# Converting the second layer's two weight matrices in turn, spread over the tiles on both sides of the layers' border

## The chip, the cores and the metric

The kernel runs on one core of one Trainium2 chip. The metric is the device time of one execution in microseconds (us). Before the change the median of three timed runs is 1086.88 us (1084.77 to 1090.79). Besides the timed runs there is one profiled execution, from which every row below is taken.

## The reference, cut to what matters

A delta-rule attention is followed by two feed-forward layers on its output. Each layer multiplies 3072 tokens of 384 features with a 384x2048 matrix, applies a function, and multiplies with a 2048x384 matrix:

```python
x = attention(q, k, v, beta)                 # 3072 tokens x 384
h = x @ moe_w_in                             # layer 1
x = (h * (1.0 / (1.0 + np.exp(-1.702 * h)))) @ moe_w_out
h = np.maximum(x @ moe2_w_in, 0.0)           # layer 2
out = (h * h) @ moe2_w_out
```

The kernel receives the four weight matrices in 64-bit form, so each must be brought to 32 bits on the chip before TensorE can use it, and each is split into a high and a low part.

## The kernel before, in words

**Tiles and steps.** The tokens are worked in six tiles of 512 per layer. A tile is 16 steps, one for each block `f` of 128 of the 2048 inner features. A step (`step`, which calls `layer2` for the step before it) gives TensorE 9 matmuls into a buffer `h` (3 blocks of features, each as high x high, low x high, high x low) and 9 matmuls into the three accumulators `z`, for the step before. Between the two lies a chain: ScalarE makes `g` from `h`, VectorE multiplies it up (`g<-g,h`), ScalarE rounds it to `ghi`, VectorE subtracts to get `glo`. There are two buffers of `h`, `g`, `ghi` and `glo`; the names in the rows carry no buffer number or, in the lists of the order, one such as `g_82` and `g_83`. TensorE's order within a step of the stretch below is three matmuls of the step's own `h`, three of the next step's `h`, three more of its own, then nine of `z`; the matmuls of the next step's `h` need a buffer that `g<-g,h` of the step before has read.

**Conversion of weights.** A matrix is converted in 16 parts of 128x384 (`split_w`). SyncE loads a part's 64-bit form into one of three buffers `raw` (`load_w`). Then ScalarE makes `c0` from it (`c<-raw` on ACT), VectorE makes two halves of `c1` (two `TENSOR_SCALAR` `c<-raw`), VectorE joins them (`c<-c,c`), ScalarE writes the high part (`vi_hi` of the first matrix of layer 2, `wo_hi` of the second), and GpSimd or VectorE, whichever the planner finds free, subtracts to get the low part (`vi_lo`, `wo_lo`). The second matrix of layer 2 takes the place of that of layer 1 in `wo_hi` and `wo_lo`, part by part, so part `f` can be written only when layer 1's last tile has used its old content. The first has storage of its own. The input of layer 2's first tile is split into `x_hi` and a low part that lies in `wi_lo`, since layer 1's first matrix is no longer needed there after four steps of the last tile.

**What sets the order.** The program does not fix the order on each engine by hand. `Program.add` collects operations with their dependencies and assumed costs; `Program.flush` then runs a plan in assumed time and issues, on each engine, the operation that is ready and was added first. An engine executes in exactly this order, and waits where a real dependency is not met. Before the change the 16 parts of the first matrix are added one behind each step of layer 1's last tile, those of the second one behind each step of layer 2's first tile. As nothing but loads, buffers and the storage holds a part back, the planner moves every part to the front as far as the three `raw` buffers allow.

Of the kernel before, what the change touches and what calls it, by code (L numbers as in the profile page):

```python
# [23 lines left out]
NF = DFF // 128  # L24
# [5 lines left out]
TUNE = dict(  # L30
    fused=4,
    warm=(10, 6),
    burst=(6, 4, 220),
    blocks=(0, 1, 2, 3),
    ja=4,
    depth=2,
    half=8,
    slack=0.0,
# [12 lines left out]
class Program:  # L51
# [8 lines left out]
    def __init__(self, queues):  # L60
        self.queues = queues
        self.ops = []
        self.writer, self.readers = {}, {}
        self.free = {q: 0.0 for q in queues}
        self.dma_free = 0.0
        self.urgent = False
        self.columns = {}
        self.run = self.run_end = self.burst_end = 0.0

    def add(self, queue, cost, fn, reads=(), writes=(), early=0, nbytes=0, after=(), cold=None):  # L70
        n = len(self.ops)
        deps = set(after)
        for k in reads:
            if k in self.writer:
                deps.add(self.writer[k])
        for k in writes:
            if k in self.writer:
                deps.add(self.writer[k])
            deps.update(self.readers.get(k, ()))
        for k in reads:  # L80
            self.readers.setdefault(k, []).append(n)
        for k in writes:
            self.writer[k], self.readers[k] = n, []
        queue = (queue,) if isinstance(queue, str) else queue
        cost = cost if isinstance(cost, tuple) else (cost,)
        self.ops.append([queue, cost, fn, deps, n - early, nbytes, None, self.urgent, cold])
# [102 lines left out]
def kernel(  # L189
# [14 lines left out]
    w1_in, w1_out, w2_in, w2_out = (w.bitcast(I32) for w in (w1_in, w1_out, w2_in, w2_out))  # L204
    pg = Program({"pe": nc.tensor, "act": nc.scalar, "dve": nc.vector, "pool": nc.gpsimd, "sp": nc.sync})
# [17 lines left out]
    wo_hi = main.tile([128, NF, DM], F32R, name="wo_hi")  # L223
    wo_lo = main.tile([128, NF, DM], F32R, name="wo_lo")
# [7 lines left out]
    NR = 3  # L232
# [73 lines left out]
    def load_w(src, f):  # L306
        s = n_conv[0] % NR
        n_conv[0] += 1
        dma(raw_sb[s], src[:, f].rearrange("p (n two) -> p n two", two=2), [], [("raw", s)], 128 * DM * 8)

    def split_w(key, f, hi, lo):
        s, t = n_conv[1] % NR, n_conv[1] % 2
        n_conv[1] += 1
        raw, c0, c1 = raw_sb[s], c0_sb[0], c1_sb[t]
        r16 = raw.rearrange("p n two -> p (n two)").bitcast(U16).rearrange("p (n q) -> p n q", q=4)
        c16 = c1.bitcast(U16).rearrange("p (n q) -> p n q", q=2)
        act(DM, [("raw", s)], ["c0"], out=c0, in_=raw[:, :, 1].bitcast(F32), scale=2.0**-112)
        ts(DM, [("raw", s)], [("c1", t, 0)], out=c16[:, :, 0], in0=r16[:, :, 1], scalar1=13, op0=ALU.logical_shift_right)
        ts(DM, [("raw", s)], [("c1", t, 1)], out=c16[:, :, 1], in0=r16[:, :, 3], scalar1=2**15, op0=ALU.bitwise_and)
        both = [("c1", t, 0), ("c1", t, 1)]  # L320
        stt(DM, ["c0"] + both, both, out=c1.bitcast(I32), in0=c0.bitcast(I32), scalar=3, in1=c1.bitcast(I32),
            op0=ALU.logical_shift_left, op1=ALU.bitwise_or)
        act(DM, both, [(key, f, 0)], out=hi[:, f, :], in_=c1)
        tt(DM, both + [(key, f, 0)], [(key, f, 1)], lo[:, f, :], c1, hi[:, f, :], ALU.subtract,
           ("pool", "dve") if n_conv[1] <= TUNE["lo_both"] else "pool")
# [363 lines left out]
    def split_x(b, c0, n):  # L689
        for c in range(KX):  # L690
            src, hi, lo = xf_sb[:, c, c0:c0 + n], x_hi[b][:, c, c0:c0 + n], x_lo[b][:, c, c0:c0 + n]
            keys = xf_keys(c, c0, n)
            K = [[("x", b, c, half, i) for half in halves_of(c0, n)] for i in range(2)]
            act(n, keys, K[0], out=hi, in_=src)
            tt(n, keys + K[0], K[1], lo, src, hi, ALU.subtract)
# [22 lines left out]
    def step(ph, j, f, c0=0, n=TT, b=0, mid=()):  # L718
        p = ns[0] % 2
        ns[0] += 1  # L720
        parts = range(2)
        if n == TT:
            ns[2] += ns[2] % 2
            s, o = ns[2] // 2 % NG, 0
            ns[2] += 2
        else:
            s, o = ns[2] // 2 % NG, CT * (ns[2] % 2)
            parts = [ns[2] % 2]
            ns[2] += 1
        W, halves = ("wi", "vi")[ph - 1], halves_of(c0, n)  # L730
        ps = h_ps[p][:, :n]
        for c in range(KX):
            wh = w_in_of[ph][0][:, f, 128 * c:128 * c + 128]
            wl = w_in_of[ph][1][:, f, 128 * c:128 * c + 128]
            hi, lo = x_hi[b][:, c, c0:c0 + n], x_lo[b][:, c, c0:c0 + n]
            mms(3 * 0.000423 * n, [(ps, wh, hi, c == 0, False), (ps, wh, lo, False, False), (ps, wl, hi, False, c == KX - 1)],
                [(W, f, 0), (W, f, 1)] + [("x", b, c, half, i) for half in halves for i in range(2)], [("h", p)])
        for todo in mid:
            todo()
        g, hi, lo = (x[s][:, o:o + n] for x in (g_sb, ghi_sb, glo_sb))  # L740
        kg, khi, klo = ([(x, s, i) for i in parts] for x in ("g", "ghi", "glo"))
        if ph == 1:
            act(n, [("h", p)], kg, out=g, in_=ps, func=AF.Tanh, scale=GATE / 2)
            stt(n, [("h", p)] + kg, kg, out=g, in0=g, scalar=1.0, in1=ps, op0=ALU.add, op1=ALU.mult)
        else:
            act(n, [("h", p)], kg, out=g, in_=ps, func=AF.Relu)
            tt(n, [("h", p)] + kg, kg, g, g, ps, ALU.mult)
        act(n, kg, khi, out=hi, in_=g)
        tt(n, kg + khi, klo, lo, g, hi, ALU.subtract)
        prev.append((ph, j, f, c0, n, hi, lo, khi + klo))  # L750
        while len(prev) > (1 if n == TT else TUNE["depth"]):
            layer2(*prev.pop(0))
# [5 lines left out]
    def convert(todo, load, n, key=None):  # L758
        for _ in range(n):
            if todo:  # L760
                _, key, f, hi, lo = todo.pop(0)
                split_w(key, f, hi, lo)
            if load:
                load_w(*(load[0][0], load.pop(0)[2]))

    with tc.manual_schedule():
# [111 lines left out]
        vi_hi = p2.tile([128, NF, DM], F32R, name="vi_hi")  # L878
        vi_lo = p2.tile([128, NF, DM], F32R, name="vi_lo")
# [6 lines left out]
        def load_z(j):  # L886
            for c in range(KX):
                dma(xf_sb[:, c], zd[128 * c:128 * c + 128, TT * j:TT * j + TT], [("zd", j, c)], xf_keys(c, 0, TT), 128 * TT * 4)

        w2i = [(w2_in, "vi", f, vi_hi, vi_lo) for f in range(NF)]  # L890
        w2o = [(w2_out, "wo", f, wo_hi, wo_lo) for f in range(NF)]
        ni, no = list(w2i), list(w2o)
        convert([], ni, NR)
        for f in range(NF):
            if f == 2:
                load_z(0)
            step(1, 5, f)
            convert(w2i, ni, 1)
        for key in [("x", 1, c, half, 1) for c in range(KX) for half in range(2)]:
            pg.readers[key] = [r for k in x_lo_keys for r in pg.readers.get(k, [])]  # L900
        split_x(1, 0, TT)
        while w2i:
            convert(w2i, ni, 1)
        for j in range(6):
            for f in range(NF):
                step(2, j, f, b=(j + 1) % 2)
                if j == 0:
                    if f == 0:
                        convert([], no, NR)
                    convert(w2o, no, 1)  # L910
                if f == 1 and j < 5:
                    load_z(j + 1)
                if f == 12 and j < 5:
                    split_x(j % 2, 0, TT)
# [69 lines left out]
```

## Time and profile before

| | |
|---|---|
| median of the runs, range | 1086.88 us, 1084.77 to 1090.79 |
| profiled execution, its own time | 1084.37 us |
| its span, first to last instruction | 1082.7 us |
| TensorE busy | 1024.4 us, 95% |
| VectorE busy | 589.6 us, 54% |
| ScalarE busy | 528.5 us, 49% |
| GpSimd busy | 332.9 us, 31% |

The time of the profiled execution is 1.67 us longer than its span. A share of busy time is a mean over stages; the share of an engine within a stage can be quite another.

### The profile page before, as it was taken

What the parts mean: (1) busy time and instruction counts of PE and PEld (TensorE: products, weight loads), DVE (VectorE), ACT (ScalarE), POOL (GpSimd) and SP (SyncE); (2) the same over time, 40 slices, a digit from 0 to 9 for tenths busy, and PEclk for the clock granted to TensorE, in tenths of its full rate; (3) what the DMA queues carried; (4) which work ended last, traced back from release to release, by engine and by line L of the source; (5) the groups of instructions that cost most, each with busy time, mean ns of one, the idle gap of its engine ahead of it and who ended that gap; (6) DMA issues with size and microseconds to landing.
All of it is one profiled execution on the core that took longest, in us unless ns stands there. A gap on an engine that the chain in (4) does not pass through costs nothing.

```text
span 1082.7 us, 23994 instructions
## 1 busy us (share of the span) xinstructions
PE 1024.4 (95%) x9900; PEld 832.9 (77%) x9900; DVE 589.6 (54%) x1122; ACT 528.5 (49%) x1088; POOL 332.9 (31%) x673
## 2 busy tenths in 40 slices
PE   4789899999999999999999989999999999999998
PEld 3778777867778787878788867788888888888886
DVE  6787886574655546453744799634333343433332
ACT  4586675636464546455544656534233242332323
POOL 1254251786647382847280144100000000000000
PEclk7798999999999999999999999999999999999999
DMA  8364462313223122212110566201001010000000
GB/s 225 98 170 133 139 174 61 113 31 93 57 60 101 60 56 88 64 51 73 50 34 5 172 179 169 94 0 59 1 7 53 1 59 1 1 30 1 30 1 29
DMA packets 43981, 76.32 MB, mean 70 GB/s; under 512 B 6624, under 2 KB 19552, under 8 KB 43872
## 3 DMA queue, kind: packets, MB, share of 16 engines
q1 hardware_dynamic: 43776, 74.75, 23.6%
q8 instruction: 77, 1.26, 0.5%
q14 instruction: 32, 0.26, 0.1%
q10 hardware_dynamic: 96, 0.05, 0.0%
HBM read 64.16 MB, written 9.44 MB: 68 GB/s over the span
## 4 chain that ended last, share of the span: by engine, by line
PE 66%; DVE 16%; ACT 8%; issue 4%; POOL 3%; DMA 2%; SPq 1%; DVEq 0%; ACTq 0%; POOLq 0%
PE h L300 28%; PE z L300 28%; PE a L300 9%; DVE c L287 3%; ACT G L273 3%; DVE kT_sb L293 2%; DVE glo L283 2%; DVE c L290 2%; DVE gu L293 1%; DVE g L290 1%; POOL tmpp L544 1%; DVE v_sb L283 1%; POOL U L547 1%; ACT gu L268 1%; DVE x_lo L283 1%
## 5 line engine op out<-in xcount | busy, mean ns | idle before, releaser
L268 ACT ACTIVATE g<-h 128x512 f32<-128x512 f32 (+1 forms) x200 | 115.5, 579 | 266.0 <-PE h L300 264.7
L300 PE MATMUL z<-glo,wo_hi 128*128 128x512 f32 (+1 forms) x600 | 231.8, 386 | 5.6 <-DVE glo L283 5.6
L300 PE MATMUL z<-ghi,wo_hi 128*128 128x512 f32 (+1 forms) x600 | 232.0, 387 | 0.1
L300 PE MATMUL z<-ghi,wo_lo 128*128 128x512 f32 (+1 forms) x600 | 229.7, 383 | 0.0
L283 DVE TENSOR_TENSOR glo<-g,ghi 128x512 fp32r<-128x512 f32 (+1 forms) x200 | 137.7, 689 | 98.6 <-ACT ghi L268 98.0
L268 ACT ACTIVATE ghi<-g 128x512 fp32r<-128x512 f32 (+1 forms) x200 | 122.6, 614 | 134.4 <-DVE g L290 68.5
L283 DVE TENSOR_TENSOR g<-g,h 128x512 f32<-128x512 f32 x96 | 66.1, 688 | 172.4 <-ACT g L268 172.4
L300 PE MATMUL h<-x_hi,wi_hi 128*128 128x512 f32 (+1 forms) x312 | 129.9, 416 | 18.3 <-DVE g L290 15.1
L544 POOL TENSOR_TENSOR tmpp<-U,gu 128x126 f32<-128x126 f32 (+22 forms) x248 | 113.2, 457 | 95.8 <-DVE U L287 77.0
L300 PEld LDWEIGHTS z<-glo,wo_hi 128*128 128x128 f32 x600 | 113.7, 189 | 33.2 <-DVE glo L283 11.8
L300 PEld LDWEIGHTS z<-ghi,wo_hi 128*128 128x128 f32 x600 | 113.6, 189 | 24.0 <-ACT ghi L268 0.9
L300 PEld LDWEIGHTS z<-ghi,wo_lo 128*128 128x128 f32 x600 | 113.7, 190 | 21.5
L290 DVE SCALAR_TENSOR_TENSOR g<-g,h 128x512 f32<-128x512 f32 (+1 forms) x104 | 66.5, 640 | 105.1 <-ACT g L268 104.9
L300 PE MATMUL h<-x_lo,wi_hi 128*128 128x512 f32 (+1 forms) x312 | 118.8, 381 | 3.2 <-DVE x_lo L283 3.2
L300 PE MATMUL h<-x_hi,wi_lo 128*128 128x512 f32 (+1 forms) x312 | 118.7, 380 | 0.4 <-DVE wi_lo L283 0.4
L300 PE MATMUL h<-x_hi,vi_hi 128*128 128x512 f32 x288 | 112.4, 390 | 0.8 <-PE h L300 0.8
L300 PE MATMUL h<-x_hi,vi_lo 128*128 128x512 f32 x288 | 112.2, 390 | 0.0
L547 POOL TENSOR_TENSOR U<-U,tmpp 128x126 f32<-128x126 f32 (+22 forms) x248 | 102.8, 415 | 20.4 <-DVE U L287 1.3
L300 PEld LDWEIGHTS h<-x_hi,wi_hi 128*128 128x128 f32 x312 | 59.7, 191 | 42.3 <-DVE g L290 24.7
L300 PEld LDWEIGHTS h<-x_hi,wi_lo 128*128 128x128 f32 x312 | 60.0, 192 | 11.6 <-DVE wi_lo L283 0.6
L300 PEld LDWEIGHTS h<-x_lo,wi_hi 128*128 128x128 f32 x312 | 60.1, 192 | 11.2 <-DVE x_lo L283 4.4
L273 ACT ACTIVATE ws<-a 32x384 f32<-32x384 f32 x92 | 44.3, 482 | 49.6 <-PE a L300 45.2
(117 smaller groups left out, 1451.4 us busy)
## 6 DMA issues: line engine op xcount, KB each, us to landing
raw<-in_w_in SPq DMA_DIRECT2D x32, 384.0 KB, 3.5
raw<-in_w_out SPq DMA_DIRECT2D x32, 384.0 KB, 3.4
kq<-in_kq SPq DMA_DIRECT2D x44, 256.0 KB, 3.0
kT_sb<-in_kq SPq DMA_DIRECT2D x11, 512.0 KB, 3.7
k_sb<-in_kt SPq DMA_DIRECT2D x12, 384.0 KB, 4.5
v_sb<-in_vt SPq DMA_DIRECT2D x12, 384.0 KB, 3.2
xf_sb<-zd SPq DMA_DIRECT2D x18, 256.0 KB, 2.7
out<-zs SPq DMA_DIRECT2D x18, 256.0 KB, 2.0
```

Of the source, the lines that this page charges most:

```text
L268: pg.add("act", c_act(n), lambda e: e.activation(**kw), reads, writes, early)
L273: e.activation(out=out, in_=in_, func=AF.Copy)
L283: pg.add(queue, cost, lambda e: e.tensor_tensor(out=out, in0=in0, in1=in1, op=op), reads, writes, early)
L287: pg.add("dve", c_dve(n, True), lambda e: e.tensor_scalar(**kw), reads, writes, early)
L290: pg.add("dve", c_dve(n), lambda e: e.scalar_tensor_tensor(**kw), reads, writes, early)
L293: pg.add("dve", c_dve(n), lambda e: e.transpose(out=out, in_=in_), reads, writes)
L300: e.matmul(out=out, lhsT=lhsT, rhs=rhs, start=start, stop=stop)
L544: e.tensor_tensor(out=t, in0=U[:, lo:hi, j:j + 1].to_broadcast(shape), in1=gu[:, j + 1:, j:j + 1].rearrange("p i o -> p o i").to_broadcast ...
L547: e.tensor_tensor(out=U[:, lo:hi, j + 1:], in0=U[:, lo:hi, j + 1:], in1=t, op=ALU.add)
```

## The change

The parts of the two matrices are put into one list in turn (first matrix part 0, second matrix part 0, first matrix part 1, ...), loaded and converted in that order. A function `spread`, called behind each step of layer 1's last tile and of layer 2's first tile (32 steps, numbered 0 to 31 here), adds the conversions that are due: part `f` of the first matrix behind step `int(1.8 f)`, part `f` of the second two steps later. That is two parts behind each of the steps 3, 5, 7, 9, 12, 14, 16, 18, 21, 23, 25 and 27, and one behind each of 0, 1, 2, 10, 11, 19, 20 and 29. While such a part is added, `gate` makes its operations depend, in the plan, on the last operation of that step. This dependency enters the plan's times alone; the conversion's instructions get no wait on a matmul from it.

```diff
+    spread=1.8,
...
+        self.gate = ()
...
-        deps = set(after)
+        deps = set(after) | set(self.gate)
...
-        w2i = [(w2_in, "vi", f, vi_hi, vi_lo) for f in range(NF)]
-        w2o = [(w2_out, "wo", f, wo_hi, wo_lo) for f in range(NF)]
-        ni, no = list(w2i), list(w2o)
-        convert([], ni, NR)
+        w2 = [x for f in range(NF) for x in ((w2_in, "vi", f, vi_hi, vi_lo), (w2_out, "wo", f, wo_hi, wo_lo))]
+        w2_load = list(w2)
+        starts = []
+
+        def spread():
+
+            starts.append(len(pg.ops) - 1)
+            while w2:
+                at = int(TUNE["spread"] * w2[0][2]) + 2 * (w2[0][1] == "wo")
+                if at >= len(starts):
+                    break
+                pg.gate = starts[at:at + 1]
+                convert(w2, (), 1)
+                pg.gate = ()
+                convert((), w2_load, 1)
+
+        convert([], w2_load, NR)
         for f in range(NF):
             if f == 2:
                 load_z(0)
             step(1, 5, f)
-            convert(w2i, ni, 1)
+            spread()
...
         split_x(1, 0, TT)
-        while w2i:
-            convert(w2i, ni, 1)
         for j in range(6):
             for f in range(NF):
                 step(2, j, f, b=(j + 1) % 2)
                 if j == 0:
-                    if f == 0:
-                        convert([], no, NR)
-                    convert(w2o, no, 1)
+                    spread()
```

The change moves rows on all engines from layer 1's last tile on. Three places on VectorE show how; names are as explained above, and `x2` stands for two instructions alike.

VectorE in steps 8 and 9 of layer 1's last tile, before the change:

```order
L290 SCALAR_TENSOR_TENSOR g_82<-g_82,h_67 128x512
L290 SCALAR_TENSOR_TENSOR c_92<-c_91,c_92 128x384
L283 TENSOR_TENSOR glo_86<-g_82,ghi_84 128x512
L287 TENSOR_SCALAR c_93<-raw_89 128x384 x2
L290 SCALAR_TENSOR_TENSOR c_93<-c_91,c_93 128x384
L287 TENSOR_SCALAR c_92<-raw_90 128x384 x2
L290 SCALAR_TENSOR_TENSOR g_83<-g_83,h_68 128x512
L290 SCALAR_TENSOR_TENSOR c_92<-c_91,c_92 128x384
L283 TENSOR_TENSOR glo_87<-g_83,ghi_85 128x512
```

The same two steps after the change:

```order
L292 SCALAR_TENSOR_TENSOR g_82<-g_82,h_67 128x512
L292 SCALAR_TENSOR_TENSOR c_92<-c_91,c_92 128x384
L285 TENSOR_TENSOR glo_86<-g_82,ghi_84 128x512
L292 SCALAR_TENSOR_TENSOR g_83<-g_83,h_68 128x512
L289 TENSOR_SCALAR c_93<-raw_88 128x384
L285 TENSOR_TENSOR glo_87<-g_83,ghi_85 128x512
L289 TENSOR_SCALAR c_93<-raw_88 128x384
L289 TENSOR_SCALAR c_92<-raw_89 128x384
L292 SCALAR_TENSOR_TENSOR c_93<-c_91,c_93 128x384
L289 TENSOR_SCALAR c_92<-raw_89 128x384
```

Before, two parts stand in every step; now two parts stand in two steps, and between `glo` of step 8 and `g` of step 9 there is nothing.

VectorE at the start of the stretch, steps 2 and 3, where the low part of layer 2's first input (`wi_lo<-xf_sb,x_hi`, three pieces) is made too, before the change:

```order
L290 SCALAR_TENSOR_TENSOR g_82<-g_82,h_67 128x512
L287 TENSOR_SCALAR c_92<-raw_88 128x384 x2
L290 SCALAR_TENSOR_TENSOR c_92<-c_91,c_92 128x384
L283 TENSOR_TENSOR glo_86<-g_82,ghi_84 128x512
L287 TENSOR_SCALAR c_93<-raw_89 128x384 x2
L290 SCALAR_TENSOR_TENSOR c_93<-c_91,c_93 128x384
L287 TENSOR_SCALAR c_92<-raw_90 128x384 x2
L283 TENSOR_TENSOR wi_lo<-xf_sb,x_hi_7279 128x512
L290 SCALAR_TENSOR_TENSOR g_83<-g_83,h_68 128x512
```

The same place after the change, from the same `g` on:

```order
L292 SCALAR_TENSOR_TENSOR g_82<-g_82,h_67 128x512
L285 TENSOR_TENSOR vi_lo<-c_92,vi_hi 128x384
L289 TENSOR_SCALAR c_92<-raw_89 128x384
L285 TENSOR_TENSOR glo_86<-g_82,ghi_84 128x512
L289 TENSOR_SCALAR c_93<-raw_88 128x384 x2
L289 TENSOR_SCALAR c_92<-raw_89 128x384
L292 SCALAR_TENSOR_TENSOR c_93<-c_91,c_93 128x384
L285 TENSOR_TENSOR wi_lo<-xf_sb,x_hi_7279 128x512 x2
L292 SCALAR_TENSOR_TENSOR c_92<-c_91,c_92 128x384
L292 SCALAR_TENSOR_TENSOR g_83<-g_83,h_68 128x512
L289 TENSOR_SCALAR c_93<-raw_90 128x384 x2
L285 TENSOR_TENSOR wi_lo<-xf_sb,x_hi_7279 128x512
```

Here the rows have not thinned out: two parts and two pieces of the input's low part now stand between one `glo` and the next `g`.

VectorE in step 23, in layer 2's first tile, where nothing but the steps' own rows stands before:

```order
L283 TENSOR_TENSOR g_83<-g_83,h_68 128x512
L283 TENSOR_TENSOR glo_87<-g_83,ghi_85 128x512
L283 TENSOR_TENSOR g_82<-g_82,h_67 128x512
L283 TENSOR_TENSOR glo_86<-g_82,ghi_84 128x512
```

The same place after the change:

```order
L285 TENSOR_TENSOR g_83<-g_83,h_68 128x512
L285 TENSOR_TENSOR glo_87<-g_83,ghi_85 128x512
L289 TENSOR_SCALAR c_93<-raw_88 128x384 x2
L289 TENSOR_SCALAR c_92<-raw_89 128x384
L292 SCALAR_TENSOR_TENSOR c_93<-c_91,c_93 128x384
L289 TENSOR_SCALAR c_92<-raw_89 128x384
L285 TENSOR_TENSOR wo_lo<-c_93,wo_hi 128x384
L292 SCALAR_TENSOR_TENSOR c_92<-c_91,c_92 128x384
L285 TENSOR_TENSOR g_82<-g_82,h_67 128x512
L285 TENSOR_TENSOR vi_lo<-c_92,vi_hi 128x384
L285 TENSOR_TENSOR glo_86<-g_82,ghi_84 128x512
```

Two parts have come in, and both of their low parts stand on VectorE; over the whole stretch VectorE has 9 of the 32 low parts now, where it had 3, and GpSimd has 23 where it had 29.

## Rows read from the trace of the kernel before

**Rows 1.** The page's 40 slices of 27 us, busy tenths.

```profile
PE   4789899999999999999999989999999999999998
DVE  6787886574655546453744799634333343433332
```

**Rows 2.** Stretch; busy us (instructions) of PE, PEld, DVE, ACT, POOL; clock; DMA share; GB/s.

```profile
613.00:688.00 75.00, 68.71 (x279) 50.62 (x278) 73.01 (x125) 47.08 (x95) 31.17 (x28) 1.00 0.62 173
688.00:763.00 75.00, 75.00 (x332) 62.10 (x331) 28.92 (x43) 28.83 (x50) 1.01 (x1) 1.00 0.09 32
```

**Rows 3.** The chain that ended last, by line, between 617 and 687 us.

```profile
by line: DVE c L287 42.3%; issue 22.7%; DVE c L290 12.2%; DVE glo L283 12.0%; DVE g L290 5.7%; DVE x_lo L283 1.9%; ACT c L268 1.6%; DVE wi_lo L283 0.9%; PE z L300 0.7%; DVEq L290 0.5%; DVEq L287 0.2%; DVEq L283 0.2%; ACT wo_hi L268 0.1%
```

**Rows 4.** VectorE's timeline through one step: start us, us, instruction.

```profile
651.73 0.68 DVE L283 TENSOR_TENSOR glo<-g,ghi 128x512 fp32r<-128x512 f32 x1
652.33 1.47 DVE L287 TENSOR_SCALAR c<-raw 128x384 uint16<-128x384 uint16 x2
653.90 0.56 DVE L290 SCALAR_TENSOR_TENSOR c<-c,c 128x384 int32<-128x384 int32 x1
654.38 0.65 DVE L287 TENSOR_SCALAR c<-raw 128x384 uint16<-128x384 uint16 x2
654.92 0.68 DVE L290 SCALAR_TENSOR_TENSOR g<-g,h 128x512 f32<-128x512 f32 x1
655.51 1.01 DVE L290 SCALAR_TENSOR_TENSOR c<-c,c 128x384 int32<-128x384 int32 x1
656.44 0.68 DVE L283 TENSOR_TENSOR glo<-g,ghi 128x512 fp32r<-128x512 f32 x1
```

**Rows 5.** GpSimd's timeline in the same step.

```profile
652.44 1.11 POOL L283 TENSOR_TENSOR wo_lo<-c,wo_hi 128x384 fp32r<-128x384 f32 x1 [1.05 <-ACT wo_hi L268]
655.10 1.00 POOL L283 TENSOR_TENSOR wo_lo<-c,wo_hi 128x384 fp32r<-128x384 f32 x1 [1.55 <-ACT wo_hi L268]
```

**Rows 6.** VectorE's `g` of step 0 and of step 16, from its timeline.

```profile
611.28 0.68 DVE L290 SCALAR_TENSOR_TENSOR g<-g,h 128x512 f32<-128x512 f32 x1
...
688.54 0.69 DVE L283 TENSOR_TENSOR g<-g,h 128x512 f32<-128x512 f32 x1
```

**Rows 7.** One undisturbed step in time, from the timelines of ScalarE, VectorE and TensorE.

```profile
703.51 0.60 ACT L268 ACTIVATE g<-h 128x512 f32<-128x512 f32 x1 [2.10 <-PE h L300]
704.14 0.69 DVE L283 TENSOR_TENSOR g<-g,h 128x512 f32<-128x512 f32 x1 [2.00 <-ACT g L268]
704.87 0.63 ACT L268 ACTIVATE ghi<-g 128x512 fp32r<-128x512 f32 x1 [0.76 <-DVE g L283]
705.53 0.69 DVE L283 TENSOR_TENSOR glo<-g,ghi 128x512 fp32r<-128x512 f32 x1 [0.70 <-ACT ghi L268]
705.98 0.39 PE L300 MATMUL h<-x_hi,vi_hi 128*128 128x512 f32 x1
707.56 0.39 PE L300 MATMUL z<-glo,wo_hi 128*128 128x512 f32 x1
```

**Rows 8.** Weight loads' waits by releaser, 605 to 695 us: us in total, times, longest.

```profile
PEld h L300 <- DVE g L290: 7.4, 12, 1.0
PEld z L300 <- DVE glo L283: 5.8, 7, 1.2
```

**Rows 9.** Instructions on tile `c`, 560 to 760 us: ns min/median/max.

```profile
L287 DVE TENSOR_SCALAR c<-raw x64: 371/389/1220, 608.2 to 687.6; 128x384 uint16<-128x384 uint16 x64
L268 ACT ACTIVATE wo_hi<-c x16: 516/527/531, 651.8 to 691.8; 128x384 fp32r<-128x384 f32 x16
L283 DVE TENSOR_TENSOR vi_lo<-c,vi_hi x2: 559/560/562, 610.8 to 614.1; 128x384 fp32r<-128x384 f32 x2
```

**Rows 10.** A piece of the input's low part, and GpSimd's instruction beside it.

```profile
626.94 1.50 DVE L283 TENSOR_TENSOR wi_lo<-xf_sb,x_hi 128x512 fp32r<-128x512 f32 x1
...
626.51 1.37 POOL L283 TENSOR_TENSOR vi_lo<-c,vi_hi 128x384 fp32r<-128x384 f32 x1 [1.05 <-ACT vi_hi L268]
```

**Rows 11.** The page's load of one part: KB, us to landing.

```profile
raw<-in_w_out SPq DMA_DIRECT2D x32, 384.0 KB, 3.4
```

## The prediction

> **What bounds the kernel now.** I first read the page's slices: VectorE rises from 4 tenths to 9 in two slices, the 24th and 25th, about 622 to 677 us, and falls back to 3, and TensorE dips to 8 in the first of the two [rows 1]. That is where layer 1's last tile runs and where the change works. The two stretches of 75 us then give the size: from 613 to 688 us VectorE is busy 73.01 us and TensorE starts 279 matmuls; in the next 75 us, with hardly any conversion left, it starts 332 at the same granted clock of 1.00 [rows 2]. A matmul takes 75 / 332 = 0.226 us there, a step of 18 takes 4.07 us, and the 53 missing ones are worth 53 x 0.226 = 12.0 us. A second count agrees: `g` of step 0 starts at 611.28 us, of step 16 at 688.54 [rows 6]; 77.26 us for 16 steps are 77.26 - 16 x 4.07 = 12.1 us too many, or 0.75 us a step.
>
> Whether VectorE causes the loss, the chain says: between 617 and 687 us its conversion lines (L287, L290 on `c`), `glo` and `g` make up over 70% of the chain, and TensorE 0.7% [rows 3]. Weight loads of TensorE wait 7.4 us for `g` and 5.8 us for `glo` there [rows 8]. One step shows how: from one `glo` to the next 4.71 us pass, filled without a gap: `glo` 0.60, a pair of halves 1.57, a join 0.48, a pair of halves 0.54, `g` 0.59, a join 0.93 [rows 4]. So two parts go through VectorE in each step, and the step lasts as long as VectorE needs. Of that, 1.03 us of the first pair and 0.45 us of the second join are excess over their other copies in the same rows, and both lie beside a low part on GpSimd, 652.44 to 653.55 and 655.10 to 656.10 [rows 4, 5]. The halves take 389 ns at the median and 1220 at most [rows 9].
>
> The Trainium skill has a rule for this (SBUF — State Buffer, section "Who interferes with whom"): VectorE and GpSimd share a port pair as an exclusive lock, and whoever comes second is blocked for the other's whole instruction. The trace agrees, 1.03 us against GpSimd's 1.11. The rule goes on to count a VectorE instruction with two SBUF inputs as a contender, and `glo` has two; what that would make of the time is the third case below.
>
> **The change part by part.** It removes nothing: 32 parts are loaded, halved, joined and rounded as before. What changes:
>
> *Six more low parts on VectorE, six fewer on GpSimd.* A low part takes 560 ns [rows 9], in a queue 0.48 like a join of the same size and duration, so 6 x 0.48 = 2.9 us more work on VectorE. It costs nothing where VectorE has room, which the next sums decide.
>
> *Work per step.* A step's own `g` and `glo` are 1.19 us [rows 4]. A part is two halves and a join: 0.54 + 0.48 = 1.02 us unblocked; blocked as in that step, 1.02 + 1.48 / 2 = 1.76. Over the 30 steps from 0 to 29 VectorE then needs 30 x 1.19 + 32 x 1.02 (to 1.76) + 9 x 0.48 + 6 x 0.60 for the pieces of the inputs' low parts = 76 to 100 us, and has 30 x 4.07 = 122. So it no longer sets the pace on the whole, and the 12.0 us are the most that can come back. What may be kept is stalls at single steps.
>
> *Slack of a step.* In an undisturbed step `g` ends at 704.83 and the matmul that needs its buffer of `h` starts at 705.98, 1.15 us later; `glo` ends at 706.22, its matmul starts at 707.56, 1.34 us later [rows 7]. TensorE stalls only by what `g` or `glo` is later than that.
>
> *Seven two-part steps that stand alone* (5, 7, 14, 16, 23, 25, 27), each followed by a step with none. Need in two steps: 2.38 + 2.04 + at most two low parts, 0.96, + 1.48 of blocking = 6.9 of 8.1 us. Of rows between `g` and `glo` there is at most one or two, and ScalarE's rounding hides 0.70 us of them [rows 7]. A `glo` held by a whole GpSimd instruction is 1.11 late, below 1.34; with a join ahead of it 1.11 + 0.48 = 1.59, 0.25 too much. I take nothing; the bound is 7 x 0.25 = 1.8 us.
>
> *The start, steps 2 and 3.* From `g` of step 2 at 0: low part 0.60, half 1.08, `glo` at 1.39 as undisturbed [rows 7], three halves to 2.80, join to 3.28, two pieces of the input to 4.48, join to 4.96, and only then `g` of step 3, due at 4.07: 0.9 us late. Halves and the third piece put `glo` at 4.96 + 0.60 + 0.54 + 0.60 = 6.70, due at 5.46: 1.24 late, within the slack. One blocked instruction adds up to 1.0 (a piece took 1.50 us instead of 0.69 beside GpSimd [rows 10]), so the stall is between 0 and 0.9; I take 0.5.
>
> *Two crowded places, steps 9 to 12 and 18 to 21,* with six parts in four steps each. Need: 4 x 1.19 + 6 x 1.02 + 2 x 0.48 = 11.8 us of 16.3, but 16.3 if every part is blocked. From nothing, then, to what four steps lose today, 4 x 0.75 = 3.0. Between the ends I go by the start's sum, nearer the lower: 0.7 each.
>
> *Loads and late users.* A load lands 3.4 us after its issue [rows 11], less than a step, and three buffers run ahead. The tightest part is the last of the second matrix: behind step 29, while its first matmul is due after step 31's `h` and 9 more matmuls, over 8 us later; halves, join, `wo_hi` (0.53 [rows 9]) and low part are some 3 us even with a wait. I take zero. Without that cover a step would wait once for the missing 1 or 2 us.
>
> **Sum.** 12.0 - 0.5 - 0.7 - 0.7 = 10.1 us won; with the bounds 12.0 at best and 12.0 - 0.9 - 3.0 - 3.0 - 1.8 = 3.3 at worst. From the profiled execution, 1084.37 (span 1082.7 and 1.67 around it), that gives 1074.3; from the median, 2.5 us higher, 1076.8. The runs scatter by more than this gap, so I forecast 1075.5.
>
> **The other ways.**
>
> *Second: the crowded places keep much of the loss.* The gain is 3.3 to 8 us, about 1080. For it: the full blocking makes VectorE's need there equal to the time. Against it: in the order the two parts of a step follow each other, so a low part on GpSimd meets the other part's rows about once, not twice.
>
> *Third: no change, for the lock moves to the steps' own rows.* Today a low part on GpSimd mostly blocks conversion rows [rows 4, 5]. With conversions thinned out it may meet `glo` or `g` instead. If each of the 23 left on GpSimd makes a step 0.5 us longer, 11.5 us go again: 1084. Against it: 1.11 us of holding is less than the slack of 1.34. It decides where a hold and a late `g` add up in most steps. The Trainium skill's rule on the shared port pair (SBUF — State Buffer, "Who interferes with whom") speaks for this case, since its two-input clause covers `glo`; no row above shows a `glo` held.
>
> *Fourth: slower.* ScalarE runs in order, and a part's `vi_hi` or `wo_hi` that waits for VectorE's join can hold the next step's `g<-h` behind it. If that ring sets a step at 4.71 us as it is today [rows 4], but now in all 31 steps up to the last part, the loss is 31 x 0.64 = 19.8 instead of 12.0: 1092. Its point is `g` more than 1.15 us late in every step, which one part per step does not make when VectorE has 1 us free in each.
>
> **Numbers.** The forecast 0.72, the second 0.15, the third 0.08, the fourth 0.05. About half a per cent, 5.4 us, is what a measurement of this kernel can tell from no change. The second straddles that line and gives 0.09 to faster and 0.06 to same: faster 0.81, same 0.14, slower 0.05. The likeliest case alone spans 1072 (all 12.0 back, from the profiled execution) to 1079; with part of the second the range goes to 1082 and leaves out the third, the fourth and a rest.
>
> **What would show it.** Right: VectorE at 6 to 8 tenths evenly from 613 to about 735 us, no slice at 9; over 320 matmuls in each 75 us from 613; step 16's `g` near 679 us instead of 688.5; TensorE back in the chain with `h` and `z`; halves mostly at 0.39 us. Stalls, if any, at steps 2 to 4, 9 to 13 and 18 to 22. Wrong: TensorE waiting for `g` or `glo` in layer 2's first tile as often as in layer 1's last today, with `glo` stretched to 1.5 us beside GpSimd (third), or ScalarE idle ahead of `vi_hi` while `g<-h` stands behind it (fourth).

## The result, and the profile after

The changed kernel takes 1074.84 us (median of 5 runs, 1073.45 to 1075.65) against 1086.88 before (median of 5, 1082.27 to 1090.79). The ratio is 0.9894 with a 95% interval of 0.9869 to 0.9918, so 9 to 14 us are won; the two medians are 12.0 us apart, the spans of the two profiled executions 1082.7 - 1072.4 = 10.3 us.

The page's slices, 26.8 us each, answer to [rows 1]:

```profile
PE   5889899999999999999999999999999999999998
DVE  7788886474655545554644477775333343433332
```

The two slices of VectorE at 9 tenths have become four at 7, and TensorE's dip is gone. The same two stretches of 75 us, with the columns of [rows 2]:

```profile
613.00:688.00 75.00, 74.80 (x329) 61.38 (x329) 57.42 (x107) 42.55 (x82) 15.85 (x14) 1.00 0.47 137
688.00:763.00 75.00, 74.70 (x327) 60.73 (x326) 45.16 (x81) 36.79 (x68) 9.49 (x10) 1.00 0.26 74
```

VectorE falls from 73.01 to 57.42 us in the first stretch and rises from 28.92 to 45.16 in the second. TensorE starts 329 matmuls instead of 279, then 327 instead of 332. Of 2 x 332 possible ones 8 are missing, 8 x 0.226 = 1.8 us; before it was 53, 12.0 us. The clock is 1.00 in all four stretches, so it has no part in this.

The chain that ended last, by line, from 617 to 687 us, is TensorE's now [rows 3], and hardly a weight load waits [rows 8]. First the head of the chain's list, then the waits from 605 to 745 us (total, times, longest):

```profile
by line: PE h L302 38.2%; PE z L302 38.1%; DVE c L289 5.2%; DVE c L292 3.8%; DVE glo L285 3.0%; DVE g L292 2.8%; issue 2.1%; ACT ghi L270 1.8%; ACT wo_hi L270 1.5%; POOL vi_lo L285 1.5%; DVE wo_lo L285 0.8%; ACT vi_hi L270 0.8%; ACT c L270 
```

```profile
PEld z L302 <- DVE glo L285: 1.6, 3, 0.5
PEld h L302 <- DVE g L285: 0.6, 2, 0.3
PEld h L302 <- DVE g L292: 0.2, 1, 0.2
```

The steps' own `g` answer to [rows 6]: step 0 at 611.25 us, step 16 at 676.18, that is 64.9 us for 16 steps instead of 77.26; the kernels below that lose no matmul, e5 and e7, take 64.3.

```profile
611.25 0.69 DVE L292 SCALAR_TENSOR_TENSOR g<-g,h 128x512 f32<-128x512 f32 x1 [3.05 <-ACT g L270]
...
676.18 0.69 DVE L285 TENSOR_TENSOR g<-g,h 128x512 f32<-128x512 f32 x1 [0.80 <-ACT g L270]
```

What is left of the loss stands where the parts stand closest. In stretches of 10 us, TensorE starts 45 or 46 everywhere from 600 to 750 us but in these two:

```profile
660.00:670.00 10.00, 9.80 (x43) 7.62 (x42) 9.55 (x18) 6.16 (x12) 2.22 (x2) 1.00 0.50 138
...
700.00:710.00 10.00, 9.71 (x42) 7.16 (x41) 8.74 (x17) 5.65 (x11) 1.11 (x1) 1.00 0.41 114
```

By the count of `g` on VectorE's timeline these are steps 12 to 14 and 21 to 23, the ends of the two crowded places.

### The profile page after: what moved, and what is told of

The parts are those of the page before. It is cut to its first block, busy times and chain, and to the rows that moved or that the text cites. A ratio compares the mean times of both kernels' runs of the same rounds, so it can differ in the third digit from the quotient of the medians.

```text
span 1072.4 us, 23975 instructions
## 1 busy us (share of the span) xinstructions
PE 1023.8 (95%) x9900; PEld 836.9 (78%) x9900; DVE 584.9 (55%) x1128; ACT 528.6 (49%) x1088; POOL 327.9 (31%) x667
## 4 chain that ended last, share of the span: by engine, by line
PE 73%; DVE 13%; ACT 7%; DMA 3%; issue 2%; SPq 1%; POOL 0%; DVEq 0%; ACTq 0%
PE h L302 32%; PE z L302 31%; PE a L302 11%; ACT G L275 2%; DVE kT_sb L295 2%; DVE gu L295 2%; DVE v_sb L285 1%; DVE c L292 1%; DVE c L289 1%; DVE g L292 1%; DVE glo L285 1%; ACT gu L270 1%; DMA kq<-in_kq 1%; SPq L257 1%; DMA raw<-in_w_out 1%
```

## The experiments

The changed kernel can have won in more than one way: because fewer parts meet in a step, because the matrices go in turn, or because less of VectorE's time is lost to GpSimd. Each kernel below differs from the kernel before or from the changed one by the edit shown; e7 and e12 join two edits. Three groups were timed apart, each beside its own runs of the kernel before; the ratio is to those runs, whose median was 1086.39 us for e1 to e4, 1085.31 for e5, e6, e9 and e11, and 1083.30 for e7, e8 and e12. Kernels of different groups are compared by ratio rather than by median. The last columns are TensorE's matmuls started between 613 and 688 and between 688 and 763 us, and the low parts and other subtractions that GpSimd runs in these 150 us. Matmuls missing are counted against 664, twice 332.

| kernel | median us | ratio, 95% interval | 613 to 688 | 688 to 763 | GpSimd |
|---|---|---|---|---|---|
| before | 1086.88 | | 279 | 332 | 29 |
| changed | 1074.84 | 0.9894, 0.9869 to 0.9918 | 329 | 327 | 23 |
| e1_no_gate | 1083.40 | 0.9977, 0.9961 to 0.9993 | 287 | 333 | 28 |
| e2_spread_1 | 1082.50 | 0.9974, 0.9957 to 0.9990 | 291 | 330 | 30 |
| e3_before_low_dve | 1073.88 | 0.9895, 0.9874 to 0.9916 | 332 | 332 | 0 |
| e4_even | 1073.25 | 0.9882, 0.9860 to 0.9905 | 330 | 333 | 16 |
| e9_before_four_c1 | 1083.86 | 0.9999, 0.9980 to 1.0018 | 282 | 332 | 28 |
| e11_low_dve_spare_pool | 1083.92 | 0.9982, 0.9960 to 1.0003 | 290 | 327 | 30 |
| e5_after_low_dve | 1072.64 | 0.9906, 0.9877 to 0.9936 | 333 | 333 | 0 |
| e6_after_low_pool | 1076.37 | 0.9931, 0.9907 to 0.9956 | 326 | 325 | 32 |
| e7_even_low_dve | 1072.07 | 0.9907, 0.9873 to 0.9941 | 333 | 333 | 0 |
| e8_one_after_other | 1072.90 | 0.9892, 0.9867 to 0.9918 | 330 | 332 | 9 |
| e12_all_low_dve | 1078.45 | 0.9954, 0.9933 to 0.9975 | 333 | 333 | 0 |

In e11 two more of its 32 subtractions on GpSimd lie before 613 us.

**The gate out, the turn kept.**

```diff
-                pg.gate = starts[at:at + 1]
```

> The changed kernel with the line that sets the gate left out: the parts are still in turn and are added behind the same steps, but the planner may pull them forward. In its order on VectorE two parts stand in nearly every step from 0 to 16. Theory A (what counts is how many parts VectorE takes per step): the stretch is as dense as in the kernel before, so the loss returns, 12 us give or take 2, a time within 3 us of the kernel before, VectorE at 9 tenths for some 65 us. Rival B (what counts is that the two matrices go in turn, so that the storage of each part comes free in time): the time stays at that of the changed kernel, about 12 us below the kernel before.

The ratio is 0.9977 and 287 matmuls start in the first stretch: theory A. Without the gate the planner packs the parts as tightly as before, and with the turn alone 44 matmuls are missing instead of 53.

**Gate and turn kept, two parts in every step.**

```diff
-    spread=1.8,
+    spread=1.0,
```

> The changed kernel with spread=1.0 for 1.8: gate and turn as in the changed kernel, but part f of each matrix is due behind step f and f+2, two parts in every step. Theory A: 32 parts in some 18 steps at 4.7 us each instead of 4.07, a loss of 10 to 12 us, so a time 0 to 3 us below the kernel before. Rival B (turn and gate do it, not the distance): the time of the changed kernel, 10 us or more below the kernel before.

291 matmuls, ratio 0.9974: theory A again. Gate and turn do little if the parts stand as close as before. Of the 43 missing matmuls not all are VectorE's doing: between 670 and 690 us the granted clock was 0.88 and then 0.95, and TensorE's first weight load of layer 2 waited 2.3 us, by the view for a low part on GpSimd.

**The kernel before, with the low parts on VectorE.**

```diff
-           ("pool", "dve") if n_conv[1] <= TUNE["lo_both"] else "pool")
+           "dve" if n_conv[1] > 2 * NF else ("pool", "dve"))
```

> The kernel before with one line changed: all 32 low parts of layer 2 on VectorE, none on GpSimd, conversions as dense as the planner likes. Theory A with the blocking by GpSimd as the larger half of a part's price: a part needs 1.02 + 0.48 = 1.50 us of VectorE instead of 1.76, two of them and a step's own 1.19 make 4.19, so the loss shrinks from 12 to 2 to 5 us and the time is 7 to 10 us below the kernel before. Rival C (VectorE's own work is the price, the blocking is hidden): 29 more low parts at 0.48 us are 13.9 us more on the engine that sets the pace, and the time is 8 to 14 us above the kernel before.

More than theory A expected: the whole loss is gone, 332 matmuls of 332, ratio 0.9895, the same as the change's, with the conversions as early as the planner puts them (done by step 19). Rival C falls. The stretch and the tile `c` of this kernel (ns min/median/max):

```profile
613.00:688.00 75.00, 75.00 (x332) 62.10 (x331) 71.71 (x162) 52.49 (x105) 0.00 (x0) 1.00 0.62 183
```

```profile
L287 DVE TENSOR_SCALAR c<-raw x64: 375/385/397, 608.0 to 686.3; 128x384 uint16<-128x384 uint16 x64
L290 DVE SCALAR_TENSOR_TENSOR c<-c,c x32: 545/551/559, 608.8 to 686.8; 128x384 int32<-128x384 int32 x32
...
L283 DVE TENSOR_TENSOR vi_lo<-c,vi_hi x16: 540/550/559, 610.6 to 649.1; 128x384 fp32r<-128x384 f32 x16
```

VectorE is busy 71.71 us of 75, hardly less than the 73.01 of before, and TensorE misses nothing. No half takes more than 397 ns, where 1220 was the longest [rows 9]. VectorE gets through 162 instructions in the stretch instead of 125: a good part of what filled it before was not work. Theory A's sum of 4.19 us is for two parts in a step; here 32 parts take some 19 steps, 1.7 in a step, which makes 1.19 + 1.7 x 1.50 = 3.7 us, below 4.07.

**One part per step.**

```diff
-                at = int(TUNE["spread"] * w2[0][2]) + 2 * (w2[0][1] == "wo")
+                at = 1 + int(0.9 * (2 * w2[0][2] + (w2[0][1] == "wo")))
```

> The changed kernel with one part per step: part number i of the list is due behind step 1 + int(0.9 i) instead of two parts behind one step. Theory A with crowding: the stalls left in the changed kernel stand in its crowded places (steps 9 to 12 and 18 to 21), so they mostly go, TensorE starts 330 or more matmuls in both stretches of 75 us from 613 us (329 and 327 in the changed kernel), and the time is 0.5 to 2 us below the changed kernel's 1074.8, about 1073.5. Rival D (the stalls come from single meetings of a low part on GpSimd with a step's own rows, wherever they stand): as many stalls at other places, time within 0.5 us of the changed kernel's.

330 and 333 matmuls, 3 missing instead of 8: the crowded places' stalls mostly go. But this edit also let the planner give VectorE 16 of the 32 low parts instead of 9, so it does not separate crowding from GpSimd, and the time cannot be told from the changed kernel's (each ratio lies in the other's interval).

**Is it waiting for GpSimd, or being blocked by it?** A low part takes 1.1 us on GpSimd and 0.56 on VectorE, so `c1` comes free later there. Four buffers of `c1` would take a wait for that away, though the waits of VectorE in the kernel before, from 605 to 690 us, name GpSimd nowhere:

```diff
+        c1_sb.extend(several(p2, "c1x", 2, [128, DM]))
...
-        s, t = n_conv[1] % NR, n_conv[1] % 2
+        s, t = n_conv[1] % NR, n_conv[1] % len(c1_sb)
```

> The kernel before with four buffers of c1 for two in layer 2's conversions; the low parts stay on GpSimd, as dense as before. Reading E (VectorE is blocked by running GpSimd instructions, inside its own): nothing is won, TensorE starts 275 to 290 matmuls between 613 and 688 us as before (279), halves still reach 1.2 us, time within 3 us of the kernel before. Reading F (moving the low parts to VectorE won because GpSimd, at 1.1 us against 0.56, held the two c1 buffers too long): with four buffers the stalls go, 325 matmuls or more, 10 us below the kernel before.

Nothing is won, 282 matmuls, ratio 0.9999: reading F falls. The sharper test adds work instead. To e3's kernel comes one subtraction on GpSimd for each part, into a tile `spare` that nobody reads:

```diff
+        if spare_sb:
+            tt(DM, [(key, f, 0)], ["spare"], spare_sb[0], hi[:, f, :], hi[:, f, :], ALU.subtract, "pool")
```

> The kernel before with all 32 low parts of layer 2 on VectorE, as in e3_before_low_dve, and besides one spare subtraction of the same size on GpSimd for each part, written to a tile that nobody reads; VectorE's order is row for row that of e3_before_low_dve and no instruction of the other engines waits for GpSimd. Reading E (blocking by running GpSimd instructions): the stalls come back and are larger than in the kernel before, since VectorE has its own low parts besides: 1.19 + 2 x (1.50 + 0.74) = 5.7 us for two parts against 4.07, a loss of 15 to 25 us, a time 3 to 13 us above the kernel before. Reading F (what counts is who waits for GpSimd): nothing waits for it, so the time stays that of e3_before_low_dve, 12 us below the kernel before.

The stalls are back, 290 and 327 matmuls, 42 + 5 missing or 10.6 us, though VectorE's order is that of e3 row for row; TensorE's weight loads wait 12.9 us for `g` and `glo` from 605 to 745 us, and once, 0.8 us, for what the view calls `spare`, where no wait for GpSimd was expected. The sizes expected were too large: a loss of 15 to 25 us and a time above the kernel before, where the ratio is 0.9982. VectorE's timeline, then GpSimd's, in the same microseconds:

```profile
650.59 0.67 DVE L283 TENSOR_TENSOR glo<-g,ghi 128x512 fp32r<-128x512 f32 x1
651.19 1.18 DVE L283 TENSOR_TENSOR vi_lo<-c,vi_hi 128x384 fp32r<-128x384 f32 x1
652.29 0.55 DVE L290 SCALAR_TENSOR_TENSOR c<-c,c 128x384 int32<-128x384 int32 x1
```

```profile
650.88 1.07 POOL L283 TENSOR_TENSOR spare<-vi_hi 128x384 fp32r<-128x384 f32 x1 [2.24 <-ACT vi_hi L268]
```

The low part lasts 1.18 us, to 652.37, beside GpSimd's instruction, which runs to 651.95; GpSimd's own takes 1.07 instead of 0.83, which fits with `glo` being in before it. Over the 32 parts (ns min/median/max, VectorE's low parts of the first matrix and GpSimd's beside them):

```profile
L283 DVE TENSOR_TENSOR vi_lo<-c,vi_hi x16: 543/1174/1183, 607.6 to 651.2; 128x384 fp32r<-128x384 f32 x16
L283 POOL TENSOR_TENSOR spare<-vi_hi x16: 826/856/2346, 607.7 to 650.9; 128x384 fp32r<-128x384 f32 x16
```

The low parts' medians are 1174 and 1170 ns, against 550 and 551 in e3: 0.62 us per meeting, and 25 of the 32 low parts are stretched. I had reckoned 0.74 and two parts per step; at e3's 32 parts in some 19 steps it is 1.19 + 1.7 x (1.50 + 0.62) = 4.8 us per step, 0.7 over 4.07, 14 us in 19 steps, and 10.6 were measured.

**The changed kernel with no low part on GpSimd, and with all of them there.** The edit is e3's line, once with `"dve"` and once with `"pool"` for the parts of layer 2.

> The changed kernel with all 32 low parts on VectorE, none on GpSimd, parts behind the same steps. Reading E: with no GpSimd instruction in the stretch, the stalls of the crowded places go though these are as crowded, 331 to 333 matmuls in both stretches of 75 us, halves at 0.37 to 0.40 us throughout, a time 0.5 to 2 us below the changed kernel, and that of e3_before_low_dve, since both then run without a stall. Against it (crowding alone stalls): VectorE has 11 us more to do, the stalls at steps 9 to 13 and 18 to 22 stay or grow, time 0 to 2 us above the changed kernel.

333 and 333 matmuls, no stall left, with the parts due behind the same steps and 23 x 0.48 = 11 us more work on VectorE. So crowding alone does not stall, and the 1.8 us that remained in the changed kernel need GpSimd too. In the time they cannot be seen: the ratio is 0.9906. Whether blocking alone makes them is not shown. Ahead of each of the two places where the changed kernel stalls, VectorE also stands idle until GpSimd is done with a low part that reads a `c1`, and e5 takes both away at once:

```profile
654.73 0.66 DVE L289 TENSOR_SCALAR c<-raw 128x384 uint16<-128x384 uint16 x2 [1.08 <-POOL vi_lo L285]
...
692.73 0.65 DVE L289 TENSOR_SCALAR c<-raw 128x384 uint16<-128x384 uint16 x2 [1.08 <-POOL vi_lo L285]
```

> The changed kernel with all 32 low parts on GpSimd, none on VectorE (9 fewer there). Reading E: VectorE saves 9 x 0.48 = 4.3 us of its own work, and 9 more GpSimd instructions block up to 0.74 us each; in the crowded places, which had low parts on VectorE, stalls grow: 1 to 3 us above the changed kernel, 324 matmuls or fewer in one of the two stretches. Against it (VectorE's own work is what counts): stalls shrink, 330 or more in both, 0 to 1.5 us below the changed kernel.

326 and 325 matmuls, 13 missing instead of 8, which is 1.1 us more: the direction that reading E gave, at the lower end of its size, though neither stretch falls to 324. The ratio of 0.9931 is the poorer one, though the two intervals overlap. Less work on VectorE makes the kernel no faster if the work goes to GpSimd.

**One part per step and no low part on GpSimd; the matrices one after the other; all 64 low parts on VectorE.** The first joins the edits of e4 and e5; the third is e4's, with `"dve"` for the low parts of both layers. The second edit is

```diff
+        w2 = [(w2_in, "vi", f, vi_hi, vi_lo) for f in range(NF)] + [(w2_out, "wo", f, wo_hi, wo_lo) for f in range(NF)]
...
+                at = w2[0][2] + 15 * (w2[0][1] == "wo")
```

> One part per step, as in e4_even, with all 32 low parts on VectorE, as in e5_after_low_dve. Reading E: each of the two alone already leaves TensorE (nearly) without a stall, so both together win nothing more: 331 to 333 matmuls in both stretches of 75 us, the time of e5_after_low_dve within 1 us, 0.5 to 2.5 us below the changed kernel. Against it: a further gain of more than 2 us would mean that the stretch still held something that the matmul counts do not show.

As reading E said: nothing beyond e5, 333 and 333 matmuls.

> The changed kernel with the two matrices one after the other instead of in turn, held back by the gate: part f of the first behind step f, of the second behind step 15 + f, one part in each step. Its low parts are shared by the planner, about half of them on VectorE. Theory A (density decides, the turn does not): the time of e4_even within 1 us, if the second matrix's parts are ready for their matmuls two steps later; if not, TensorE waits for wo_hi or wo_lo in layer 2's first tile, up to 1 us in each of 16 steps. Rival B (the turn itself wins): 5 us or more above e4_even.

330 and 332 matmuls, ratio 0.9892: the turn is not needed, and with parts due two steps ahead of their use TensorE's waits name no `wo_hi` and no `wo_lo`. The planner put 23 of the 32 low parts on VectorE, more than the half expected.

> As e7_even_low_dve, with the 32 low parts of layer 1 on VectorE too (16 of them are on GpSimd in the others), in the stage from 26 to 200 us where VectorE also serves the attention. Reading E alone says that 16 GpSimd instructions fewer block VectorE for up to 16 x 0.6 = 10 us less, against 16 x 0.48 = 8 us more of its own: a change between -3 and +1 us against e7_even_low_dve. If VectorE's own work sets the pace of that stage, up to 8 us more.

Outside reading E's range: 1078.45 against e7's 1072.07, 6.4 us slower by the medians and 5 by the ratios, whose intervals just touch, where -3 to +1 was expected, and up to 8 if VectorE's own work counts there. Layer 1's stage has VectorE at work for the attention too. The granted clock between 100 and 200 us was 0.93 against 0.98 in e7's profile, but e4, with e7's instructions there, had 0.94. First e12, then e7:

```profile
100.00:200.00 100.00, 91.22 (x1639) 76.05 (x1635) 74.73 (x171) 61.82 (x147) 27.34 (x63) 0.93 0.37 114
```

```profile
100.00:200.00 100.00, 92.81 (x1762) 77.68 (x1758) 76.30 (x165) 65.07 (x155) 38.74 (x79) 0.98 0.41 120
```

Whether the work or the clock is the cause was not tried and stays open; the lesson of layer 2's stretch does not carry over to layer 1's as it stands.

## Why the prediction was right

**The size.** The forecast was 1075.5 us and 1074.84 was measured. The working gave 10.1 us back; the counts of matmuls give (53 - 8) x 0.226 = 10.2, the two profiled spans 10.3. The medians lie 12.0 apart, but the runs behind them scatter over 2 us after and 9 us before the change.

**What bounds the stretch.** Right. The 12.0 us at stake, counted from 53 missing matmuls, are confirmed by e3, e5 and e7, which lose none and lie 11 to 13 us below the kernel before by their medians, 10 to 11 by their ratios.

**The price of a part, and GpSimd's share of it.** The working put 1.48 us of two parts' 3.52 down to GpSimd. The runs go further. Without this share the same 32 parts in the same 80 us cost nothing (e3), and with GpSimd's instructions added back beside VectorE's unchanged order the stalls return (e11). Density sets how much of it is felt: GpSimd runs 29 low parts in the kernel before and 32 in e6, and 53 matmuls are missing where the parts are packed, 13 where they are spread. Two things happen. Fewer instructions meet: VectorE's instructions that last over 0.1 us longer than the median of their form do so by 18.7 us in all in the kernel before (28 of them), 12.2 in e6 (23) and 9.5 in the changed kernel (15), added up from the traces between 604 and 760 us. And of what is left, the steps' slack takes most. So the change won by thinning out and cushioning the meetings, and would have had nothing to win without them. The prediction said that VectorE no longer sets the pace because its need falls from all of the time to 76 to 100 us of 122; in that sum the excess was a side term to two parts per step, and it is the main one. Its own prices say so: two unblocked parts and a step's rows are 2 x 1.02 + 1.19 = 3.2 us, which fit into 4.07.

**The third case, blocking that reaches the steps' own rows.** A low part took 1.18 us beside GpSimd against 0.55 without, and of the 34 `glo` in the stretch one took 1331 ns against a median of 693, beside a low part on GpSimd that began 0.65 us earlier. That is what the Trainium skill says (SBUF — State Buffer, section "Who interferes with whom"): a VectorE instruction with two SBUF inputs contends with GpSimd's reads, and the later one is held; the trace agrees. `g<-g,h`, whose second input is in PSUM, never took more than 690 ns. Here are the changed kernel's rows on `g` (ns min/median/max), and the one long `glo` with GpSimd's instruction beside it:

```profile
L285 DVE TENSOR_TENSOR glo<-g,ghi x34: 677/693/1331, 607.5 to 744.6; 128x512 fp32r<-128x512 f32 x34
L292 DVE SCALAR_TENSOR_TENSOR g<-g,h x17: 673/683/690, 606.1 to 672.7; 128x512 f32<-128x512 f32 x17
L285 DVE TENSOR_TENSOR g<-g,h x17: 678/687/689, 676.2 to 742.8; 128x512 f32<-128x512 f32 x17
```

```profile
674.05 1.33 DVE L285 TENSOR_TENSOR glo<-g,ghi 128x512 fp32r<-128x512 f32 x1
...
673.40 1.44 POOL L285 TENSOR_TENSOR vi_lo<-c,vi_hi 128x384 fp32r<-128x384 f32 x1 [1.05 <-ACT vi_hi L270]
```

So the third case's mechanism exists, once in 34 here and 5 times in 37 in e6, and no weight load of the changed kernel waits there: the slack of 1.34 us absorbs it. That case fell on its size.

**Slack and places of the stalls.** Steps 5, 7 and the other lone pairs: no stall, as taken. The start, steps 2 and 3: 0.5 was taken, none is seen; `g` of step 3 starts 5.02 us after that of step 2 (622.82 and 617.80), 0.95 late as worked out, and stays within 1.15. The two crowded places: 0.7 us each was taken; in the stretch of 10 us around each TensorE starts 3 or 4 matmuls too few, some 0.7 and 0.9 us. In sum 1.9 was taken for the rest of the loss, and 1.8 measured; that they come so close is partly luck, since the start lost nothing and the crowded places lost a little more than taken.

The places were also not quite as pictured. The list is worked in its order, so a part of the first matrix comes no earlier than the part of the second that stands ahead of it: by the program its parts 1, 6 and 11 follow steps 2, 11 and 20, not 1, 10 and 19. The crowded places are therefore two steps with two parts each, 11 and 12, and 20 and 21, after a step with none, and the stalls stand right behind them, in steps 12 to 14 and 21 to 23. The prediction's six parts in four steps are right, its spread of them over the four is not.

VectorE's timeline at the first of them, and GpSimd's beside it, show the two blocked pairs that the bound was made of:

```profile
659.84 0.68 DVE L292 SCALAR_TENSOR_TENSOR g<-g,h 128x512 f32<-128x512 f32 x1
660.43 1.48 DVE L289 TENSOR_SCALAR c<-raw 128x384 uint16<-128x384 uint16 x2
662.02 0.56 DVE L292 SCALAR_TENSOR_TENSOR c<-c,c 128x384 int32<-128x384 int32 x1
662.50 0.69 DVE L285 TENSOR_TENSOR glo<-g,ghi 128x512 fp32r<-128x512 f32 x1
663.10 1.48 DVE L289 TENSOR_SCALAR c<-raw 128x384 uint16<-128x384 uint16 x2
664.68 0.56 DVE L292 SCALAR_TENSOR_TENSOR c<-c,c 128x384 int32<-128x384 int32 x1
665.16 0.68 DVE L292 SCALAR_TENSOR_TENSOR g<-g,h 128x512 f32<-128x512 f32 x1
```

```profile
660.56 1.11 POOL L285 TENSOR_TENSOR vi_lo<-c,vi_hi 128x384 fp32r<-128x384 f32 x1 [5.87 <-ACT vi_hi L270]
663.22 1.11 POOL L285 TENSOR_TENSOR wo_lo<-c,wo_hi 128x384 fp32r<-128x384 f32 x1 [1.54 <-ACT wo_hi L270]
```

From `g` to `g` 5.32 us pass instead of 4.07, the whole slack and a little more.

**The six more low parts on VectorE** were costed at nothing where it has room. Right, and too cautious: e5 moves 23 more and starts 10 matmuls more in the two stretches.

**Loads and late users.** No wait for `wo_hi` or `wo_lo` stands among TensorE's, and none for `raw` among those of VectorE and ScalarE from 605 to 745 us; costed at nothing rightly, and e8 shows that two steps are enough.

**The fourth case**, ScalarE holding `g<-h` behind a rounding, did not come as feared, every step, but its sign stands in the crowded places. At the first, ScalarE waits for VectorE's join ahead of `wo_hi`, and `g<-h` of steps 12 and 13 follows without idle time. Counted in steps of 4.07 us from 654.54, where `g<-h` of step 11 starts, they are 0.6 and 0.8 us late:

```profile
658.34 0.53 ACT L270 ACTIVATE wo_hi<-c 128x384 fp32r<-128x384 f32 x1 [1.28 <-DVE c L292]
...
659.20 0.58 ACT L270 ACTIVATE g<-h 128x512 f32<-128x512 f32 x1
...
662.62 0.53 ACT L270 ACTIVATE wo_hi<-c 128x384 fp32r<-128x384 f32 x1 [1.16 <-DVE c L292]
...
663.49 0.58 ACT L270 ACTIVATE g<-h 128x512 f32<-128x512 f32 x1
```

These `g<-h` end at 659.78 and 664.07, and VectorE comes to `g<-g,h` only at 659.84 and 665.16, so VectorE's own rows were the later ones.

## What to carry to other kernels

An instruction that lasts longer than its copies in the same view can hide a wait that no list of waits shows; look which instruction of another engine runs beside it, and price that, before calling the engine full. Work handed to GpSimd to relieve VectorE can cost VectorE more than doing it: here 0.62 us lost per meeting against 0.48 us for doing the low part itself. In this stretch, spreading such work and taking it back to VectorE are two ways to the same 12 us. Taking it back alone returns all of them (e3), spreading alone all but 2.9 (e6, 13 matmuls); e3's single line and the changed kernel cannot be told apart by time. In layer 1's stage, taking it back did not pay (e12).

## What the runs showed that was not expected

VectorE at 71.71 us of 75, 95% busy, held up nothing in e3: a queue that is nearly full is no bound while each `g` and `glo` comes within its slack.

The first 100 us vary from run to run, although all kernels but e12 have the same instructions there: the granted clock in the profiles is 0.76 in e1 and 0.77 in e4 and 0.83 in e2 and e6. e4's profiled span is 1077.0 us although its stretch has fewer stalls than the changed kernel's with 1072.4. A span of one profile therefore says less about the change than the count of matmuls in the stretch that it touches.

```profile
0.00:100.00 100.00, 75.31 (x1448) 66.18 (x1450) 77.58 (x224) 59.95 (x150) 34.03 (x64) 0.77 0.54 157
```

The line above is e4's; the changed kernel's is this:

```profile
0.00:100.00 100.00, 76.14 (x1531) 66.83 (x1533) 80.12 (x226) 62.85 (x158) 35.80 (x69) 0.80 0.56 165
```
